# Weight preparation of a blockwise FFT convolution: ten transformed taps by TensorE, or seven by TensorE and three sums by VectorE

## The chip, the cores and the metric

One NeuronCore of a Trainium2 chip runs the whole program. The metric is the device time of one execution in microseconds (us). Engines are called as in the profile: PE is TensorE's matmul and PEld its weight load, DVE is VectorE, ACT is ScalarE, POOL is GpSimd, SP is SyncE, which issues the DMAs.

## The reference

A circular 7 x 7 convolution of a 224 x 224 image with 96 channels in and 96 out, written with FFTs. Input and output are bf16.

```python
wp = jnp.pad(w, ((0, H - K), (0, W - K), (0, 0), (0, 0)))
Xf = rfft2(x.astype(float32), axes=(1, 2))
Wf = rfft2(wp.astype(float32), axes=(0, 1))
Yf = jnp.einsum('bhwi,hwio->bhwo', Xf, Wf)
y = irfft2(Yf, s=(H, W), axes=(1, 2)).astype(bfloat16)
```

## The kernel before, in words

The kernel transforms the rows' axis only, in 8 blocks of 28 rows with windows of 34 (17 frequencies after a real DFT), and convolves directly along the columns, with 7 taps. The columns are worked in 7 tiles of 32 (16 even, 16 odd).

**Tables.** `WF[96 in, 50 slots, taps, 96 out]` holds the transformed weights. Frequency 0 has two slots, each other frequency three: parts 0 and 1 and their difference, part 2, so that a complex product takes three real ones. Even and odd columns are split in the same manner: the products need the even taps 0, 2, 4, 6, the odd taps 1, 3, 5, and the sums 0+1, 2+3, 4+5 (with 6). Before the change these sums are taps 7, 8 and 9 of the same table (`TAPS`, line 29).

**Weight preparation** (`prep_jobs`, lines 312 to 348) is done in groups of frequencies, `PGRP`. The raw weights `wq` are the stationary operand (98 rows: 49 taps by two halves of the output channels), and the moving operand is `Em`, a DFT table in which each column picks its slot and tap. One matmul gives, for one pair of output channels, all slots and taps of the group. Several of them fill a bank of PSUM (`pb`); one copy (CAST) then moves the bank into `WF`. For the groups after the first, TensorE makes parts 0 and 1 only, and `diff(s)` makes part 2 on VectorE, one TENSOR_TENSOR a frequency.

**Who copies.** `evac` (line 116) keeps a running cost for DVE and ACT and gives each copy to the engine with the lower sum; `diff` adds its cost to DVE's.

**Order.** Every engine runs its instructions in the order in which the program issues them (`_Ordered`). At the start come tile 0's row transform for frequencies 0 to 7, filler matmuls on `wu`, group 0's weights (`prep_jobs(0)`, line 679), then more of the row transform and the first J planes (`jit`, line 685). Then rounds r = 0 to 20 follow (line 727): in round r tile 0 works on frequency r and tile 1 on frequency r - 4. In `b_round` (line 466) a frequency goes like this:

- matmuls `pb<-WF,J` and `pb<-WF,xf` into bank b0 (19 of 96 columns), whose first four use taps 7, 8, 9, 6;
- ACT copies part of b0 to `tt_` (ACTIVATE), then DVE makes `u` from b0 and `tt_`;
- `mid()`: filler jobs; then 14 matmuls into bank b1; DVE makes `v`;
- J planes for three later frequencies on DVE, if due (three TENSOR_TENSOR: 1824, 456 and 912 elements);
- POOL (from tile 2 on sometimes DVE) adds v and u into `yf`; after planes, that sum waits for them; `end()`: filler jobs.

The filler jobs are the row transform of the next tiles and the weights of the next group: group g is spread over the rounds of the frequencies of group g - 1 (line 715), evenly by `pace`. `tt_`, u and v have two buffers each, and all matmul results share 8 PSUM banks, so PE can be only a few banks ahead of the copies. A group is due before the first of its frequencies is convolved.

After a tile's 17 frequencies, `yf` goes through DRAM (`scr`) and comes back transposed (`tt`); matmuls with `Gm` do the inverse DFT, ACT copies to `yo`/`J`, SP stores. From round 14 on no weights are prepared.

The tile's first pixels lie in the last slots of `WF` (`late`, line 155) until the last group's weights overwrite them.

Of the kernel before, what the change touches and what calls it, by code (L numbers as in the profile page):

```python
# [8 lines left out]
BF16 = mybir.dt.bfloat16  # L9
F32 = mybir.dt.float32  # L10
ALU = mybir.AluOpType
ACTF = mybir.ActivationFunctionType

KT = 7
# [8 lines left out]
TW = 16  # L23
HALO = 3
PXC = 16
NB = 8
POS = TW + HALO
NTAP = 10
TAPS = ((7, 8, 9, 6), (0, 2, 4, 6), (1, 3, 5))
NSLOT = 2 + 3 * (NS - 1)  # L30
PGRP = ((0, 2), (2, 5), (5, 8), (8, 11), (11, 14), (14, 17))
YGRP = ((0, 3), (3, 6), (6, 9), (9, 12), (12, 15), (15, 17))
YGRPL = ((0, 3), (3, 6), (6, 9), (9, 12), (12, 15), (15, 17))
SA = 9
# [13 lines left out]
def slot(s, part):  # L48
    return part if s == 0 else 2 + 3 * (s - 1) + part
# [3 lines left out]
def kernel(  # L53
# [7 lines left out]
    _, H, W, C = x.shape  # L61
# [4 lines left out]
    R = HB + PAD  # L66
# [3 lines left out]
    C2 = C // 2  # L70
# [21 lines left out]
    VE, SE, GE, TE, DE = (_Ordered(e) for e in (nc.vector, nc.scalar, nc.gpsimd, nc.tensor, nc.sync))  # L92

    cpool = ctx.enter_context(tc.tile_pool(name="const", bufs=1))
# [10 lines left out]
    load = {"v": 0.0, "a": 0.0}  # L105
# [3 lines left out]
    def apart(key, zone, r):  # L109
        for z, q in parts.setdefault(key, []):  # L110
            if z != zone and q.engine != r.ins.engine:
                tc.declare_no_dep(r.ins, q, reason="disjoint parts of one tile")
        parts[key].append((zone, r.ins))
        return r

    def evac(out_ap, in_ap, n):
        if tail[0]:
            return tail_evac(out_ap, in_ap, n)
        cv, ca = 180 + 1.0 * n, 160 + 0.85 * n
        if load["v"] + cv <= load["a"] + ca:  # L120
            load["v"] += cv
            return VE.tensor_copy(out=out_ap, in_=in_ap)
        load["a"] += ca
        return SE.copy(out=out_ap, in_=in_ap)
# [6 lines left out]
        return DE.dma_start(out=out_ap, in_=in_ap)  # L131

    WF = cpool.tile([128, NSLOT, NTAP, C], BF16, name="WF")
    PP = POS * NJ
    JN = 7 * 3 * PP
    J_bufs = [cpool.tile([128, JN], BF16, name=f"J{i}") for i in range(3)]
# [6 lines left out]
    XW = 2 * TW * C  # L143
# [8 lines left out]
    WC = C * C - C2  # L152
    Em = wqx[0:PW2, WC:WC + 2 * NSLOT * NTAP].rearrange("p (h a t) -> p h a t", h=2, a=NSLOT)
    XHW = PAD * C + 32
    late = WF[0:R, NSLOT - 8:NSLOT].rearrange("p a t o -> p (a t o)")
    x0_bufs = [late[:, i * (XW + 32):(i + 1) * (XW + 32)] for i in range(2)]
    xh_bufs = [late[:, 2 * (XW + 32) + i * XHW:2 * (XW + 32) + (i + 1) * XHW] for i in range(2)]
    assert 2 * (XW + 32 + XHW) <= 8 * NTAP * C and NSLOT - 8 > slot(PGRP[-1][0], 0)

    def load_rows(xb, jg, w0, npx):  # L160
        h0 = jg * HB - PAD
# [53 lines left out]
    twc = ftile([PW2, KT]); mf = ftile([R, JG, NS * 2])  # L215
# [31 lines left out]
    floor_div(GE, twp[:], pm[:], 2)  # L247
    GE.tensor_single_scalar(out=th14[:], in_=twp[:], scalar=-2.0, op=ALU.mult)
    GE.tensor_tensor(out=hf[:], in0=th14[:], in1=pm[:], op=ALU.add)
    GE.tensor_scalar(out=mk[:, 0:KT], in0=twc[:], scalar1=twp[:, 0:1], scalar2=None, op0=ALU.is_equal)  # L250
    GE.tensor_tensor(out=mk[:, KT:NTAP], in0=mk[:, 0:6:2], in1=mk[:, 1:6:2], op=ALU.add)
    GE.tensor_scalar(out=mk2[:, 1], in0=mk[:], scalar1=hf[:, 0:1], scalar2=None, op0=ALU.mult)
    GE.tensor_tensor(out=mk2[:, 0], in0=mk[:], in1=mk2[:, 1], op=ALU.subtract)
    for xb in xh_bufs:
# [3 lines left out]
    for xb in xf_bufs:  # L258
# [3 lines left out]
                     in1=mf.rearrange("p j (s r) -> p j s r", r=2), op=ALU.mult)  # L262
# [7 lines left out]
    for k0, k1 in ((0, slot(PGRP[0][1], 0)), (slot(PGRP[0][1], 0), NSLOT)):  # L270
        VE.tensor_tensor(out=Em[:, :, k0:k1], in0=pe3[:, k0:k1].unsqueeze(1).unsqueeze(3).to_broadcast([PW2, 2, k1 - k0, NTAP]),
                         in1=mk2[:].unsqueeze(2).to_broadcast([PW2, 2, k1 - k0, NTAP]), op=ALU.mult)
# [39 lines left out]
    def prep_jobs(gi):  # L312
        s0, s1 = PGRP[gi]
        ns = s1 - s0
        full = gi == 0
        ncol = (NSLOT_OF(s0, s1) if full else 2 * ns) * NTAP
        nb = C // NB
        hb = NB // 2
        assert NB * ncol <= 512 and C2 % hb == 0

        def mk_(ob):
            def f():
                pw = bank()
                pv_ = pw[:, 0:NB * ncol].rearrange("p (k h q) -> p k h q", h=2, q=ncol)
                ev = Em[:, :, slot(s0, 0):slot(s1 - 1, 2) + 1, :]
                ev = ev.rearrange("p h a t -> p h (a t)") if full else ev.rearrange("p h (s r) t -> p h s (r t)", r=3)[:, :, :, 0:2 * NTAP]
                for k in range(hb):
                    o = ob * hb + k
                    TE.matmul(pv_[:, k], lhsT=wqx[0:PW2, o:o + 127 * C + 1:C], rhs=ev, start=True, stop=True)
                pv_ = pv_[0:C]  # L330
                o0, o1 = ob * hb, (ob + 1) * hb
                wv = WF[0:C, slot(s0, 0):slot(s1 - 1, 2) + 1]
                if full:
                    wv = wv.rearrange("i a t (h o) -> i (a t) h o", h=2)
                    apart(("W", gi), ob, evac(wv[..., o0:o1], pv_.rearrange("i k h q -> i q h k"), NB * ncol))
                    return
                wv = wv.rearrange("i (s r) t (h o) -> i s (r t) h o", r=3, h=2)
                apart(("W", gi), ob, evac(wv[:, :, 0:2 * NTAP, :, o0:o1],
                      pv_.rearrange("i k h (s q) -> i s q h k", s=ns), NB * ncol))
            return f  # L340

        def diff(s):
            def f():
                load["v"] += 60 + C * NTAP / 1.92
                w0, w1, w2 = (WF[0:C, slot(s, r)].rearrange("i t o -> i (t o)") for r in range(3))
                VE.tensor_tensor(out=w2, in0=w0, in1=w1, op=ALU.subtract)
            return f
        return [mk_(ob) for ob in range(nb)] + ([] if full else [diff(s) for s in range(s0, s1)])

    def NSLOT_OF(s0, s1):  # L350
        return slot(s1 - 1, 2) + 1 - slot(s0, 0)
# [114 lines left out]
    def b_round(t, s, mid, end, ydve=False, planes=()):  # L466
# [14 lines left out]
        def conv(bank, col, m, part, add=False, both=False):  # L481
            pl = st[m][part] if s > 0 else (xv[:, 0, :, 0], Jb[:, 2:4], Jb[:, 0:2])[m][:, part]
            tp = TAPS[m]
            for k, tp_ in enumerate(tp):
                o, wv = bank[:, col:col + C], WF[0:C, slot(s, part), tp_, :]
                if both:
                    o, wv = bank[:, col:col + 2 * C].rearrange("p (m o) -> p m o", m=2), wv.unsqueeze(1).to_broadcast([C, 2, C])
                TE.matmul(o, lhsT=pl[:, (HALO - k) * NJ:(HALO - k) * NJ + 128], rhs=wv,
                          start=(k == 0 and not add), stop=(k == len(tp) - 1 and not both and m != 2 or not add and not both and k == len(tp) - 1))
# [3 lines left out]
        if s == 0:  # L493
# [4 lines left out]
            for mi, m in enumerate((2, 1)):  # L498
                for part in range(2):
                    conv(b1, (mi * 2 + part) * C, m, part)  # L500
            VE.tensor_tensor(out=yv.rearrange("p r m o -> p m r o"),
                             in0=tt_[:, 0:2 * C].rearrange("p (r o) -> p r o", o=C).unsqueeze(1).to_broadcast([128, 2, 2, C]),
                             in1=b1[:, 0:4 * C].rearrange("p (m r o) -> p m r o", m=2, r=2), op=ALU.add)
# [5 lines left out]
        else:  # L509
            v = tv_pool.tile([128, 2, 2, C], F32, name="v")  # L510
# [368 lines left out]
```

## Time and profile before

| What | Value |
|---|---|
| Runs | 279.18, 280.52, 283.91 us; median 280.52 |
| Span of the profiled execution | 279.9 us (first to last instruction; it is the only time of that execution) |
| Mean granted TensorE clock | 0.981 |
| Instructions | 12291 |
| `pb<-wq` matmuls | 240 of 98x120 and 48 of 98x100 (columns of the moving operand last) |
| CAST `WF<-pb` on ACT | 52 of 480 elements, mean 578 ns; 6 of 400, mean 495 ns |
| CAST `WF<-pb` on DVE | 8 of 480, mean 646 ns; 6 of 400, mean 571 ns |
| TENSOR_TENSOR `WF<-WF` (diff) on DVE | 15 of 960, mean 752 ns |
| TENSOR_TENSOR `J<-xf` in four runs of 304 | 7 of 1216, mean 831 ns |
| TENSOR_TENSOR `yf<-v,u` on POOL | 85 of 384 (f32 in), mean 1012 ns |
| First weight matmul, first convolution matmul | 17.49 us, 22.03 us |

Nearly all instructions carry line 85, a helper's, so groups are told apart by their tiles: `WF<-pb` is written out of PSUM, `pb<-wq` is the weight transform, `pb<-Fm,xn` the row transform. A row of the time order has start, length, engine, operation, tiles, shape, count, and in brackets the idle time before it with what ended that. Consecutive equal instructions are merged into one row, so a row's length divided by its count is less than one instruction's length where they overlap.

### The profile page before, as it was taken

The page shows a single profiled execution, that of the slowest core. Times are in us where ns is not written, and L with a number is a line of the kernel's source. Part 1 is how long each engine was busy: PE and PEld are TensorE (multiplying, and loading weights), DVE is VectorE, ACT ScalarE, POOL GpSimd, SP SyncE. Part 2 cuts the span into 40 slices and gives each one's busy share as a digit, 9 for nine tenths or more (in the row PEclk, how much of TensorE's full clock was granted, in tenths as well). Part 3 has the DMA queues.
Part 4 walks back from the last instruction along what each step waited for, and adds up shares of the span by engine and source line. Part 5 has one row for each costly group of instructions (what it writes and reads, how often), then busy time and mean ns, then how long its engine had stood idle before and what let it go on. Part 6 is the DMA issues. An engine that isn't in the chain of part 4 may idle for free. (4 is left out here: it accounts for less than half of the span.)

```text
span 279.9 us, 12291 instructions
## 1 busy us (share of the span) xinstructions
PE 266.0 (95%) x5226; PEld 243.6 (87%) x5226; DVE 218.9 (78%) x457; ACT 199.0 (71%) x489; POOL 98.1 (35%) x146
## 2 busy tenths in 40 slices
PE   8989999999999999999999999999999996999791
PEld 3769999999999999999999999999999896989571
DVE  6547999889798798879887887789788798588232
ACT  5439996687964667988988699887989864574022
POOL 7720132453446654224223334322422333133000
PEclk9999999999999999999999999999999999799797
DMA  6947010812111597897977596989299339756935
GB/s 184 213 108 205 11 47 2 248 52 85 44 47 46 163 261 143 251 251 208 263 192 222 143 298 183 266 247 298 82 204 281 114 108 207 204 158 164 251 65 165
DMA packets 46038, 46.79 MB, mean 167 GB/s; under 512 B 35150, under 2 KB 36954, under 8 KB 45886
## 3 DMA queue, kind: packets, MB, share of 16 engines
q1 hardware_dynamic: 43696, 43.94, 57.9%
q10 hardware_dynamic: 2288, 2.06, 2.6%
q8 instruction: 41, 0.67, 1.1%
q14 instruction: 13, 0.11, 0.1%
HBM read 24.65 MB, written 21.33 MB: 164 GB/s over the span
## 5 line engine op out<-in xcount | busy, mean ns | idle before, releaser
L85 PE MATMUL pb<-WF,J 96*128 96x96 bf16 x2898 | 168.4, 206 | 0.9 <-DVE WF L85 0.3
L85 PEld LDWEIGHTS <-J 96*128 96x128 bf16 x2898 | 143.0, 98 | 10.6 <-issue 1.5
L85 POOL TENSOR_TENSOR yf<-v,u 128x384 bf16<-128x384 f32 x85 | 84.6, 1012 | 150.0 <-issue 102.0
L85 ACT CAST xf<-pb 96x408 bf16<-96x408 f32 (+2 forms) x147 | 68.5, 486 | 6.7 <-PE pb L85 4.6
L85 PE MATMUL pb<-WF,xf 96*128 96x96 bf16 x952 | 60.6, 207 | 1.2 <-DVE WF L85 0.6
L85 DVE TENSOR_TENSOR J<-xf 96x1824 bf16<-96x1824 bf16 (+1 forms) x84 | 60.0, 753 | 0.1
L85 PEld LDWEIGHTS <-xf 96*128 96x128 bf16 x952 | 47.4, 98 | 1.6 <-issue 1.0
L85 PE MATMUL pb<-Fm,xn 118*128 118x136 bf16 (+3 forms) x640 | 45.7, 199 | 0.4 <-DVE u L85 0.4
L85 PE MATMUL pb<-tt,Gm 102*84 102x384 bf16 (+1 forms) x132 | 32.8, 329 | 2.2 <-DMA tt<-scr 2.2
L85 ACT CAST WF<-pb 96x480 bf16<-96x480 f32 (+1 forms) x58 | 28.5, 569 | 6.8 <-PE pb L85 6.7
L85 ACT CAST J<-pb 84x384 bf16<-84x384 f32 (+1 forms) x66 | 28.3, 482 | 6.1 <-PE pb L85 3.1
L85 PEld LDWEIGHTS <-xn 118*128 118x128 bf16 x640 | 30.5, 97 | 0.5 <-issue 0.5
L85 ACT CAST yo<-pb 84x384 bf16<-84x384 f32 (+1 forms) x66 | 28.1, 480 | 4.0 <-PE pb L85 3.9
L85 DVE TENSOR_TENSOR J<-J 96x912 bf16<-96x912 bf16 (+1 forms) x42 | 25.0, 595 | 0.0
L85 PE MATMUL pb<-wq 98*128 98x120 bf16 (+1 forms) x288 | 21.5, 226 | 0.9 <-DMA wq<-in_w_dram 0.9
L85 PE MATMUL pb<-wu 128*128 128x512 bf16 (+1 forms) x80 | 20.2, 422 | 1.0 <-DVE ct L85 1.0
L85 PEld LDWEIGHTS <-wq 98*128 98x128 bf16 x288 | 19.5, 151 | 1.3 <-DMA wq<-in_w_dram 1.3
L85 PEld LDWEIGHTS <-wu 128*128 128x128 bf16 (+1 forms) x80 | 10.4, 132 | 9.7 <-issue 3.5
L85 DVE TENSOR_TENSOR yf<-v,u 128x384 bf16<-128x384 f32 x27 | 15.5, 574 | 0.9
L85 PEld LDWEIGHTS <-Gm 102*84 102x84 bf16 (+1 forms) x132 | 11.1, 118 | 3.0 <-DMA tt<-scr 2.4
L85 DVE CAST WF<-pb 96x480 bf16<-96x480 f32 (+1 forms) x14 | 8.1, 614 | 7.0 <-PE pb L85 6.9
L85 ACT CAST tt<-pb 112x384 bf16<-112x384 f32 x8 | 3.6, 480 | 11.9 <-PE pb L85 11.8
(391 smaller groups left out, 236.2 us busy)
## 6 DMA issues: line engine op xcount, KB each, us to landing
scr<-yf SPq DMA_DIRECT2D x30, 288.0 KB
xn<-in_x_dram SPq DMA_DIRECT2D x12, 672.0 KB
tt<-scr SPq DMA_DIRECT2D x24, 336.0 KB
out_dram<-yo SPq DMA_DIRECT2D x12, 252.0 KB
out_dram<-J SPq DMA_DIRECT2D x12, 252.0 KB
tt<-scr SPq DMA_DIRECT2D x6, 288.0 KB
wq<-in_w_dram SPq DMA_DIRECT2D x1, 1719.0 KB
WF<-in_x_dram SPq DMA_DIRECT2D x2, 672.0 KB
```

Source lines behind the costliest of these rows:

```text
L85: r = fn(*a, **k)
```

## The change

TensorE transforms 7 taps instead of 10: `Em`, `WF` and the group tables shrink, and a bank of PSUM holds more channels or more frequencies. The groups become 2, 3, 4, 4 and 4 frequencies instead of 2, 3, 3, 3, 3 and 3. The matmuls per bank are set by group (`HBK`: 6, 6, 4, 4, 4 instead of 4), the banks per group become 8, 8, 12, 12 and 12 instead of 12 each. The three sums go to a table of their own, `WS`, by one TENSOR_TENSOR a frequency on VectorE (`tapsum`), which follows that frequency's `diff`: 864 elements, 576 for frequency 0. The convolution reads taps 7 to 9 from `WS`. The overlay `late` moves to the last 12 slots. `tapsum` adds its cost to the running cost by which `evac` chooses.

```diff
-NB = 8
-NTAP = 10
+NTAP = 7
+NSUM = 3
-PGRP = ((0, 2), (2, 5), (5, 8), (8, 11), (11, 14), (14, 17))
+PGRP = ((0, 2), (2, 5), (5, 9), (9, 13), (13, 17))
+HBK = (6, 6, 4, 4, 4)
...
+    WS = cpool.tile([128, NSLOT, NSUM, C], BF16, name="WS")
...
-    late = WF[0:R, NSLOT - 8:NSLOT].rearrange("p a t o -> p (a t o)")
+    late = WF[0:R, NSLOT - 12:NSLOT].rearrange("p a t o -> p (a t o)")
...
-    GE.tensor_scalar(out=mk[:, 0:KT], in0=twc[:], scalar1=twp[:, 0:1], scalar2=None, op0=ALU.is_equal)
-    GE.tensor_tensor(out=mk[:, KT:NTAP], in0=mk[:, 0:6:2], in1=mk[:, 1:6:2], op=ALU.add)
+    GE.tensor_scalar(out=mk[:], in0=twc[:], scalar1=twp[:, 0:1], scalar2=None, op0=ALU.is_equal)
...
-        nb = C // NB
-        hb = NB // 2
-        assert NB * ncol <= 512 and C2 % hb == 0
+        hb = HBK[gi]
+        nb = C2 // hb
+        assert 2 * hb * ncol <= 512 and C2 % hb == 0
...
-        return [mk_(ob) for ob in range(nb)] + ([] if full else [diff(s) for s in range(s0, s1)])
+
+        def tapsum(s):
+            def f():
+                a0, a1 = slot(s, 0), slot(s, 1 if s == 0 else 2) + 1
+                load["v"] += 60 + (a1 - a0) * C * NSUM / 1.92
+                VE.tensor_tensor(out=WS[0:C, a0:a1], in0=WF[0:C, a0:a1, 0:2 * NSUM:2], in1=WF[0:C, a0:a1, 1:2 * NSUM:2], op=ALU.add)
+            return f
+        jobs = [mk_(ob) for ob in range(nb)]
+        for s in range(s0, s1):
+            jobs += ([] if full else [diff(s)]) + [tapsum(s)]
+        return jobs
...
-                o, wv = bank[:, col:col + C], WF[0:C, slot(s, part), tp_, :]
+                o, wv = bank[:, col:col + C], WF[0:C, slot(s, part), tp_, :] if tp_ < NTAP else WS[0:C, slot(s, part), tp_ - NTAP, :]
```

More of the change, by code (lines that the diff above doesn't have):

```diff
@@ L154 @@
     XHW = PAD * C + 32
-    late = WF[0:R, NSLOT - 8:NSLOT].rearrange("p a t o -> p (a t o)")
+    late = WF[0:R, NSLOT - 12:NSLOT].rearrange("p a t o -> p (a t o)")
     x0_bufs = [late[:, i * (XW + 32):(i + 1) * (XW + 32)] for i in range(2)]
     xh_bufs = [late[:, 2 * (XW + 32) + i * XHW:2 * (XW + 32) + (i + 1) * XHW] for i in range(2)]
-    assert 2 * (XW + 32 + XHW) <= 8 * NTAP * C and NSLOT - 8 > slot(PGRP[-1][0], 0)
+    assert 2 * (XW + 32 + XHW) <= 12 * NTAP * C and NSLOT - 12 >= slot(PGRP[-1][0], 0)
     def load_rows(xb, jg, w0, npx):
@@ L323, in f @@
                 pw = bank()
-                pv_ = pw[:, 0:NB * ncol].rearrange("p (k h q) -> p k h q", h=2, q=ncol)
+                n = 2 * hb * ncol
+                pv_ = pw[:, 0:n].rearrange("p (k h q) -> p k h q", h=2, q=ncol)
                 ev = Em[:, :, slot(s0, 0):slot(s1 - 1, 2) + 1, :]
@@ L334, in f @@
                     wv = wv.rearrange("i a t (h o) -> i (a t) h o", h=2)
-                    apart(("W", gi), ob, evac(wv[..., o0:o1], pv_.rearrange("i k h q -> i q h k"), NB * ncol))
+                    apart(("W", gi), ob, evac(wv[..., o0:o1], pv_.rearrange("i k h q -> i q h k"), n))
                     return
@@ L338, in f @@
                 apart(("W", gi), ob, evac(wv[:, :, 0:2 * NTAP, :, o0:o1],
-                      pv_.rearrange("i k h (s q) -> i s q h k", s=ns), NB * ncol))
+                      pv_.rearrange("i k h (s q) -> i s q h k", s=ns), n))
             return f
```

## The prediction

> **What bounds the kernel now.** I read the page's first part, then busy time by stretches, then the time order of single engines. The first part:
>
> ```profile
> PE 266.0 (95%) x5226; PEld 243.6 (87%) x5226; DVE 218.9 (78%) x457; ACT 199.0 (71%) x489; POOL 98.1 (35%) x146
> ```
>
> TensorE (PE) is busy for 95% of the span, so a matmul less is time less wherever nothing else is late. VectorE's 78% is a mean. The stretches in which the weights are prepared (width, then busy us of PE, weight load, DVE, ACT, POOL, then clock):
>
> ```profile
> 30.00:50.00 20.00, 19.07 (x457) 18.77 (x457) 19.73 (x36) 16.63 (x43) 5.90 (x6) 1.00 0.11 35
> 50.00:82.00 32.00, 32.00 (x734) 31.91 (x732) 27.41 (x54) 24.39 (x57) 13.91 (x15) 1.00 0.29 93
> 82.00:97.00 15.00, 14.92 (x397) 14.78 (x394) 12.29 (x29) 8.81 (x23) 10.18 (x12) 1.00 0.24 76
> ```
>
> From 30 to 50 us DVE is busy 19.73 of 20 us, more than PE. From 50 to 82 us PE is full and DVE has 4.6 us idle. The time order of PE, in the places the change touches:
>
> ```profile
> 17.49 3.15 PE L85 MATMUL pb<-wq 98*128 98x100 bf16 x48 [0.87 <-DMA wq<-in_w_dram]
> ...
> 22.38 1.45 PE L85 MATMUL pb<-wq 98*128 98x120 bf16 x20
> ...
> 24.07 0.76 PE L85 MATMUL pb<-WF,J 96*128 96x96 bf16 x14
> ```
>
> ```profile
> 41.97 0.33 PE L85 MATMUL pb<-WF,xf 96*128 96x96 bf16 x4 [0.36 <-DVE WF L85]
> ...
> 46.73 0.55 PE L85 MATMUL pb<-Fm,xn 118*128 118x32 bf16 x16 [0.38 <-DVE u L85]
> ```
>
> One matmul lasts about 0.2 us but the next starts long before its end. The last two rows carry the forecast: at 41.97 and 46.73 PE stands and waits for DVE. And DVE, from which the rest is priced:
>
> ```profile
> 28.70 1.21 DVE L85 CAST WF<-pb 96x480 bf16<-96x480 f32 x2
> 29.95 1.79 DVE L85 TENSOR_TENSOR WF<-WF 96x960 bf16<-96x960 bf16 x3
> 31.66 0.54 DVE L85 SCALAR_TENSOR_TENSOR v<-tt__643,pb 128x384 f32<-128x384 f32 x1
> 32.12 1.41 DVE L85 TENSOR_TENSOR J<-xf 96x1824 bf16<-96x1824 bf16 x2
> 33.45 0.62 DVE L85 TENSOR_TENSOR J<-J 96x912 bf16<-96x912 bf16 x1
> ...
> 40.51 2.55 DVE L85 TENSOR_TENSOR WF<-WF 96x960 bf16<-96x960 bf16 x3
> ...
> 43.91 1.96 DVE L85 TENSOR_TENSOR J<-xf 96x1824 bf16<-96x1824 bf16 x2
> ...
> 46.34 0.34 DVE L85 SCALAR_TENSOR_TENSOR u<-pb,tt__1130 128x192 f32<-128x192 f32 x1
> ```
>
> ```profile
> 40.40 1.00 POOL L85 TENSOR_TENSOR yf<-v,u 128x384 bf16<-128x384 f32 x1 [3.92 <-DVE J L85]
> 43.60 0.99 POOL L85 TENSOR_TENSOR yf<-v,u 128x384 bf16<-128x384 f32 x1 [2.20 <-DVE v L85]
> ```
>
> No DVE row from 29.95 to 48.49 us has idle time before it: it is one unbroken chain. The same three differences take 1.79 us at 29.95 and 2.55 at 40.51, where POOL's sum is running; the two J rows take 1.41 and, beside the next POOL sum, 1.96.
>
> **The change part by part.** Counts are from the instruction order of the two built kernels.
>
> *TensorE.* Each group has 48 matmuls, and six groups become five: 288 become 240. At 100 columns they start (3.15-0.22)/47 = 62 ns apart, at 120 columns (1.45-0.23)/19 = 64 ns, where 0.22 is one matmul's length; the convolution's 96 columns take (0.76-0.21)/13 = 42 ns. So the width does not set the 62 ns, and I give nothing for 70, 84 or 112 columns: 48 x 62 ns = -3.0 us. Bounds: 42 ns each, -2.0; or also 10 ns less on the 96 narrow ones, -4.0. Groups 0 to 2 keep 48 matmuls each, at the same times, so the saving falls after round 5 (47 us).
>
> The Trainium skill (TensorE: Matmul & The Clock Gate, Back-to-back issue gap) has the gap follow the columns, N/2.4 + 2.5 ns; by it the estimate would be 14.7 us before, 10.4 after, -4.3. The rows above contradict it: 100 and 120 columns cost the same.
>
> *VectorE, new prices.* Bf16 sums: 1.10 us for 1824 elements, 0.39 for 456, 0.65 for 960, so 0.52 ns an element; 672 elements (a difference now) 0.50, 864 (a tap sum) 0.60. Independent ones start 0.07 to 0.08 us before the end of the one ahead ((1.79-0.65)/2 = 0.57 apart). A tap sum reads the difference just ahead of it, and such a reader starts after the end: the casts that began at 28.70 ended at 29.91, the difference started at 29.95. So a pair takes 0.50 + 0.03 + 0.52 = 1.06 us where a difference took 0.57. Bounds for the tap sum, whose rows of 96 lie apart: 0.60 by the dense rows, and 1.02 at the rate of v and u (0.54 and 0.35 us for 384 and 192 elements, 0.99 ns each). Taken: 0.60, since J with four separate runs of 304 (1216 elements) has a mean of 0.83. Casts cost (1.21-0.65) = 0.57 apart at 480 elements, 0.54 at 448.
>
> *Rounds 1 to 5, on the path.* Between v at 31.66 and u at 46.34 DVE gets four casts of 0.54 for two of 0.57 (+1.0) and, in round 4, four pairs for three differences (4.24 - 1.71 = +2.5): 3.5 us. Beside POOL it already loses 0.76 + 0.55 us; I keep that. Bounds: 1.8 (no wait inside a pair, one collision less), 5.2 (the dear tap sum). The chain's start: DVE now adds two tap sums (0.37 + 0.52) behind the last cast before J, a third xf copy goes to ACT, and the first convolution starts about 0.6 later; round 1 then has one cast and three pairs (0.60 + 3.2) for four casts and three differences (2.3 + 1.7) and the 1.60 us that DVE waited for ACT at 28.43. I get v at 28.43 + 0.9 + 0.27 + 2.1 = 31.7, unchanged (plus or minus 0.5). Behind the pairs stand u, v and J of the next rounds. PE waits on that u at 46.73 with no slack, so PE is late by **+3.5**.
>
> *Rounds 5 to 13.* DVE loses two casts, one xf copy and nine differences (1.1 + 0.6 + 5.1) and gets eight pairs (8.5): +1.6. Its idle time there is 0.3 + 4.6; with PE 3.0 faster 1.9 stays, so the pairs just fit. Taken **+0.3**; bounds 0, and 2.0 for new collisions.
>
> The Trainium skill (GPSIMD Engine Reference, Specifications) says that GpSimd shares its SBUF interfaces with VectorE and contends with instructions that have two SBUF inputs. The 2.55 row agrees, and it speaks against 32 such instructions in place of 15; a full sum's wait for each new one would be an estimate of 17 us, none would be 0.
>
> *Edits at nothing.* ACT has 43 casts for 58, and is nowhere PE's releaser there. The shorter weight table product (1.1 us) and the longer zero fill lie before 17.46 us, where PE waits for the weights' DMA: that cover holds as long as both end before it. SP's order of DMAs is unchanged, so no queue moves; POOL's two memsets (0.19 and 0.28) come two sums earlier, under its idle time. After round 13 nothing differs.
>
> *Sum.* 279.9 span - 3.0 + 3.5 + 0.3 = 280.7. The median of the runs, 280.52, is 0.6 above this span (runs 279.18 to 283.91), so the forecast for a median is **281.3**, no change.
>
> **The rivals.**
> 1. PE's saving shows. If the pairs have no inner wait, the chain starts 0.5 earlier and a collision goes, u is late by 1.3 instead of 3.5: 279.1. For it: ACT and DVE together lose 15 + 5 casts. Against it: DVE has no idle between 29.95 and 48.49.
> 2. Slower: collisions with POOL's sums in rounds 7 to 12. Each difference or tap sum that starts behind a v falls on a 1.0 us POOL sum and loses up to 0.76. With 1.9 - 1.6 = 0.3 us spare, it decides from the second collision on; eight pairs give 8 x 0.76 = 6.1, less 0.8 already paid (the nine differences there have the row mean 0.75, not 0.65): 286.6. Against it: a DVE that waits for PE before u meets POOL already done.
> 3. Tap sums at one element a cycle: 0.42 each, four before u and eight behind: +5.0, 286.3. The J row with four runs speaks against it.
> 4. The clock drops. After PE's one wait of 2.2 us for tt at 236.75 the granted clock read 0.64 and 0.51 from 238 to 242; a wait of 3 us at 42 to 47 might do the same: about 3.4 us at half speed, +1.7, 283.0. The shorter waits at 41.97 and 46.73 left it at 1.00.
>
> **How the numbers follow.** Forecast 0.45, rival one 0.22, two 0.13, three 0.07, four 0.13. The likeliest case alone spans 279.7 to 282.9. The range 278.3 to 285.5 leaves out rival three, half of two and the far end of one, below 0.2. Two per cent (274.9 and 286.1) is about what a measurement of this kernel can tell from no change. Faster by that needs more than the 4.0 us that PE can save: 0.03. Slower: most of three, half of two: 0.13. Within: 0.84.
>
> **What would show it.** 240 matmuls on wq, about 62 ns apart; pairs 1.06 us apart; the u behind the fourth group of J rows near 50 us and PE's wait in front of it 3 to 4 us instead of 0.5; from 50 to 85 us PE gaining 3 us. Wrong would be: wq matmuls below 55 ns, tap sums over 0.75 us, DVE with idle time between 32 and 48 us, or a clock under 1.00 near 50 us.

## The result, and the profile after

The changed kernel takes **292.25 us** (median of 4 runs, 291.33 to 293.69) against 280.13 us before (4 runs, 279.18 to 283.91): 1.043 times as long, 95% interval 1.039 to 1.048. The forecast was 281.3 us, no change, with a range to 285.5. The profiled execution has a span of 290.9 us and took 292.58 us. Medians in this document are over all runs of a kernel, ratios leave out those over 1.5% above its fastest and compare with runs of the kernel before taken alongside (medians 280.8 to 281.5 us), and a profile is of one run, for instance in e8 the fastest, in e4, e9 and e16 the slowest of its kernel.

The first part of the page of the changed kernel, and its row of the TensorE clock in 40 slices of 7.3 us:

```profile
PE 267.1 (92%) x5178; PEld 245.8 (85%) x5178; DVE 225.5 (78%) x467; ACT 194.1 (67%) x476; POOL 97.8 (34%) x145
...
PEclk9997996895997899999999999999999999999998
```

The shares look almost as before: DVE at 78% again, PE three points lower. What is new stands in the second row: the clock dips four times in the first 14 slices, where before it dipped in none. The same stretches as in the prediction show where (columns as there, the clock behind the five engines):

```profile
30.00:50.00 20.00, 16.74 (x393) 16.43 (x390) 19.48 (x36) 14.07 (x37) 4.22 (x4) 0.90 0.05 18
50.00:82.00 32.00, 29.36 (x606) 29.22 (x604) 24.00 (x48) 19.82 (x47) 10.99 (x11) 0.85 0.27 84
82.00:97.00 15.00, 10.50 (x208) 10.36 (x205) 14.19 (x27) 4.65 (x13) 6.03 (x7) 0.78 0.11 42
```

PE was full from 50 to 97 us before; now it lacks 7.1 us of 47, and what it does there is partly done at half clock (0.85 and 0.78). DVE is nearly unbroken from 82 to 97 us, and yet has 8 us idle from 50 to 82.

In the time order of PE four waits stand out; the brackets have the idle time before the row and what ended it:

```profile
44.35 0.30 PE L86 MATMUL pb<-WS,J 96*128 96x96 bf16 x3 [1.62 <-DVE WS L86]
...
48.25 1.28 PE L86 MATMUL pb<-WF,J 96*128 96x96 bf16 x14 [1.63 <-DVE v L86]
...
67.02 0.42 PE L86 MATMUL pb<-WS,J 96*128 96x96 bf16 x3 [2.63 <-ACT xf L86]
...
91.95 0.42 PE L86 MATMUL pb<-WS,J 96*128 96x96 bf16 x3 [4.50 <-DVE J L86]
```

Three such matmuls take 0.30 us at 44.35 and 0.42 at 67.02 and 91.95, fourteen take 1.28 us at 48.25 (0.76 before): half clock. The row at 67.02 names ACT, but the matmul reads J planes, and the second row of planes on DVE (456 elements, merged into the "x2" row at 65.55) ends at 66.9. What DVE did before 91.95:

```profile
84.42 0.54 DVE L86 SCALAR_TENSOR_TENSOR v<-tt__1938,pb 128x384 f32<-128x384 f32 x1
84.89 0.35 DVE L86 SCALAR_TENSOR_TENSOR u<-pb,tt__1994 128x192 f32<-128x192 f32 x1
85.15 1.35 DVE L86 TENSOR_TENSOR WS<-WF 96x864 bf16<-96x864 bf16 x1
86.43 0.49 DVE L86 TENSOR_TENSOR WF<-WF 96x672 bf16<-96x672 bf16 x1
86.96 0.60 DVE L86 TENSOR_TENSOR WS<-WF 96x864 bf16<-96x864 bf16 x1
87.48 0.54 DVE L86 SCALAR_TENSOR_TENSOR v<-tt__1994,pb 128x384 f32<-128x384 f32 x1
87.95 0.35 DVE L86 SCALAR_TENSOR_TENSOR u<-pb,tt__2050 128x192 f32<-128x192 f32 x1
88.21 1.25 DVE L86 TENSOR_TENSOR WF<-WF 96x672 bf16<-96x672 bf16 x1
89.50 0.60 DVE L86 TENSOR_TENSOR WS<-WF 96x864 bf16<-96x864 bf16 x1
90.02 0.54 DVE L86 SCALAR_TENSOR_TENSOR v<-tt__2050,pb 128x384 f32<-128x384 f32 x1
90.49 1.40 DVE L86 TENSOR_TENSOR J<-xf 96x1824 bf16<-96x1824 bf16 x2
```

```profile
85.04 1.00 POOL L86 TENSOR_TENSOR yf<-v,u 128x384 bf16<-128x384 f32 x1 [1.97 <-DVE v L86]
88.11 0.99 POOL L86 TENSOR_TENSOR yf<-v,u 128x384 bf16<-128x384 f32 x1 [2.06 <-DVE v L86]
```

The bunch of a group's pairs stands in front of v and of the J planes. An instruction of a pair that starts just after GpSimd has begun a sum takes 1.25 to 1.35 us instead of 0.49 to 0.60; it ends 0.4 to 0.5 us after that sum's end. PE is meanwhile as far ahead as the planes allow, and stands still for 4.5 us.

In the rest of the text, as in the expectations, a wait of PE is counted from the start of its last matmul, which makes it 0.2 us longer than the idle time in the brackets (1.8, 1.8, 2.8 and 4.7 us here).

**Where the time went.** VectorE makes one v per frequency and tile, so the n-th v is the same instruction in all kernels. The 1st, 5th, 21st and 35th v start at 31.66, 46.60, 81.70 and 105.61 us before. I call the stretches between them *rounds 1 to 5*, *rounds 5 to 13* and *behind*. "Late" is the delay of the 35th v ("at 118 us" in the expectations below) against the first profile of before; the delay then stays within 0.7 us until 232 us. A second profile of each of the two kernels is in the table too.

| Late by (us) | start | rounds 1 to 5 | rounds 5 to 13 | behind | 35th v |
|---|---|---|---|---|---|
| before again (b2) | -0.25 | 0.0 | 0.0 | 0.0 | -0.2 |
| changed | 1.2 | 3.4 | 7.5 | 2.7 | 14.9 |
| changed again (a2) | 1.1 | 3.4 | 8.0 | 2.8 | 15.4 |
| no sums (e1) | 0.0 | 1.0 | -1.6 | 0.4 | -0.2 |
| groups of three (e2) | 1.6 | 1.6 | 7.3 | 1.6 | 12.1 |
| pairs in time (e3) | 0.3 | 2.7 | 3.6 | 3.0 | 9.5 |
| filled waits (e4) | 1.1 | 3.4 | 6.3 | 0.8 | 11.6 |
| half the sums (e8) | -0.3 | 2.2 | 1.4 | 1.9 | 5.2 |
| GpSimd copies (e10) | 0.8 | 2.4 | 6.6 | 1.5 | 11.3 |
| pairs ahead of the sum (e12) | -0.2 | 3.6 | 1.4 | 3.7 | 8.4 |
| before in that order (e13) | -0.7 | 2.7 | -0.8 | 2.3 | 3.6 |
| e12, half the sums (e16) | -1.1 | 2.3 | 0.6 | 3.0 | 4.7 |
| e12, no sums (e15) | -0.4 | 0.2 | -2.6 | 2.0 | -0.7 |

Rounds 5 to 13 hold eight pairs wherever VectorE makes all sums (nine in e2). In e3, e6, e7, e12, e13, e15 and e16 two or three pairs or differences move into the stretch "behind", which makes it longer.

Of the 14.9 us, 3.9 are not in the span. That goes with the clock records of the 20 profiles: between 232 us and the last half clock, which ends each run, both profiles of before have two pieces of 3.41 us at half clock and the changed kernel's first has none. The eleven profiles with none regain 3.9 to 5.9 us there, the six with one piece 1.8 to 3.4, the two with two nothing, and e4 with three loses 1.0. With the second profiles (293.5 and 279.8 us) the difference is 13.7. I therefore judge mechanisms by the table, which repeats within 0.6 us, and the time by medians.

### The profile page after: what moved, and what is told of

It is laid out like the page before. It is cut to its first block, busy times and chain, and to the rows that moved or that the text cites. A ratio compares the mean times of both kernels' runs of the same rounds, so it can differ in the third digit from the quotient of the medians.

```text
span 290.9 us, 12194 instructions
## 1 busy us (share of the span) xinstructions
PE 267.1 (92%) x5178; PEld 245.8 (85%) x5178; DVE 225.5 (78%) x467; ACT 194.1 (67%) x476; POOL 97.8 (34%) x145
## 4 chain that ended last, share of the span: by engine, by line
PE 70%; DVE 12%; DMA 9%; ACT 4%; issue 2%; SPq 1%; DVEq 0%; ACTq 0%
PE pb L86 70%; DMA wq<-in_w_dram 5%; DVE J L86 3%; DVE v L86 2%; ACT xf L86 2%; DVE WF L86 2%; DVE WS L86 2%; DMA xf<-scrb 2%; DMA tt<-scr 2%; DVE u L86 1%; DVE yf L86 1%; ACT WF L86 1%; DMA scrb<-yf 1%; SPq L86 1%; DVE xf L86 0%
## 5 line engine op out<-in xcount | busy, mean ns | idle before, releaser
L86 PE MATMUL pb<-WF,J 96*128 96x96 bf16 x2562 | 162.4, 209 | 2.0 <-DVE v L86 1.6
L86 PEld LDWEIGHTS <-J 96*128 96x128 bf16 x2898 | 146.3, 99 | 20.6 <-DVE J L86 7.7
L86 ACT CAST xf<-pb 96x408 bf16<-96x408 f32 (+3 forms) x149 | 69.2, 483 | 7.3 <-PE pb L86 5.4
L86 PE MATMUL pb<-WS,xf 96*128 96x96 bf16 x714 | 56.4, 209 | 1.5 <-ACT ct L86 1.4
L86 PE MATMUL pb<-WF,xf 96*128 96x96 bf16 x238 | 45.7, 209 | 0.0
L86 PE MATMUL pb<-WS,J 96*128 96x96 bf16 x336 | 33.5, 209 | 8.8 <-DVE J L86 4.5
L86 ACT CAST WF<-pb 96x448 bf16<-96x448 f32 (+2 forms) x43 | 20.7, 546 | 8.8 <-PE pb L86 8.7
L86 PE MATMUL pb<-wq 98*128 98x112 bf16 (+2 forms) x240 | 18.5, 239 | 1.1 <-DMA wq<-in_w_dram 1.1
L86 PE MATMUL pb<-wu 128*128 128x512 bf16 (+1 forms) x80 | 17.8, 385 | 1.0 <-DVE ct L86 1.0
L86 PEld LDWEIGHTS <-wq 98*128 98x128 bf16 x240 | 17.1, 156 | 1.5 <-DMA wq<-in_w_dram 1.5
```

Source lines behind the costliest of these rows:

```text
L86: r = fn(*a, **k)
```

## The experiments

Theory at the start: the tap sums on VectorE hold up v, u and the J planes, PE waits, and each wait halves the clock. First rival: not the sums but the regrouping to four frequencies does it.

**e1_no_sums**, the sums left out.

```diff
-        jobs = [mk_(ob) for ob in range(nb)]
-        for s in range(s0, s1):
-            jobs += ([] if full else [diff(s)]) + [tapsum(s)]
-        return jobs
+        return [mk_(ob) for ob in range(nb)] + ([] if full else [diff(s) for s in range(s0, s1)])
...
-                o, wv = bank[:, col:col + C], WF[0:C, slot(s, part), tp_, :] if tp_ < NTAP else WS[0:C, slot(s, part), tp_ - NTAP, :]
+                o, wv = bank[:, col:col + C], WF[0:C, slot(s, part), tp_ if tp_ < NTAP else 2 * (tp_ - NTAP), :]
```

> The changed kernel with its 17 tap sums left out: the convolution reads taps 0, 2 and 4 of WF in the place of the sums, so that part of the computation is missing. Theory: the sums on VectorE, issued in front of v, u and the J planes, cause PE's four long waits (1.8, 1.8, 2.8 and 4.7 us at 42.5, 46.4, 64.2 and 87.3 us), and each wait is followed by a half clock. Without the sums I expect no PE wait above 1 us from 30 to 97 us, a granted clock of 1.00 there and 276 to 279 us (280.1 before, less the 3.0 us of matmuls). Rival, the regrouping: four differences in one bunch and banks of another size hold up the rounds by themselves; then 285 us or more.

277.17 us (10 runs), 0.992 of before (0.986 to 0.997); clock 1.00 from 20 to 110 us, longest wait there 1.2 us (1 expected). The sums are the cause, not the regrouping.

**e2_groups_of_three**, the sums kept, the old groups.

```diff
-PGRP = ((0, 2), (2, 5), (5, 9), (9, 13), (13, 17))
-HBK = (6, 6, 4, 4, 4)
+PGRP = ((0, 2), (2, 5), (5, 8), (8, 11), (11, 14), (14, 17))
+HBK = (6, 6, 6, 6, 6, 6)
...
```

> The changed kernel with the groups of frequencies of before (2, 3, 3, 3, 3, 3; six matmuls to a bank, 8 banks a group), sums kept. PE gets its 48 matmuls back (+3.0 us). Theory (the sums): the waits remain, in shorter bunches of three pairs, 286 to 294 us, a clock below 1.00 in at least one stretch between 30 and 97 us. Rival (the regrouping): 280 to 283 us with the clock at 1.00.

291.79 us, 1.041 (1.031 to 1.052), four half-clock stretches of 3.4 us between 47 and 99 us: the theory again. PE waits in more and shorter pieces, six of 0.8 to 1.4 us.

**e3_pairs_in_time**, one pair a round.

```diff
...
+    later = []
     for gi in range(1, len(PGRP)):
-        add(2 * PGRP[gi - 1][0], 2 * PGRP[gi - 1][1] - 1, prep_jobs(gi))
+        banks, prs = prep_jobs(gi)
+        a = 2 * PGRP[gi - 1][0]
+        b = max(2 * PGRP[gi - 1][1] - 2, a + 3)
+        add(a, b, banks)
+        later += [(max(2 * s - 2, b - 1), p) for s, p in prs]
+    for k, p in later:
+        add(k, k + 1, p)
```

> The changed kernel with the same work, but difference and tap sum of a frequency s are issued in round s-1, one pair a round, in place of all pairs of a group in the last rounds of the group before; the last three pairs so move behind round 12. Theory, refined: it is the bunching in front of the J planes that makes the waits. Then no PE wait above 2 us from 30 to 97 us, at most one half-clock stretch, 278 to 283 us. Rival: the amount of VectorE work in rounds 1 to 13 counts and not where it stands; then PE's waits come elsewhere and the time stays above 288 us.

287.18 us, 1.028 (1.017 to 1.038), between the two, with waits of 2.7 and 2.2 us, where I expected none above 2, and two half-clock stretches, where I expected at most one. Rounds 5 to 13 lose 3.6 us instead of 7.5: the bunches cost about 4. But a pair now starts behind u in each round, beside a sum of GpSimd, and its rows, with those of J, are 8.0 us longer than the shortest of their kind (changed kernel 5.4).

**e4_filled_waits**, filler matmuls in front of four banks.

```diff
+FILL = {(0, 5, 0): 8, (0, 5, 1): 8, (0, 9, 0): 12, (1, 9, 0): 20}
...
+    def fill_wait(b, key):
+        for _ in range(FILL.get(key, 0)):
+            TE.matmul(b[:].rearrange("p (a b) -> p a b", a=4), lhsT=wu[:, 0:128], rhs=wur, start=True, stop=True)
...
+            fill_wait(b0, (t, s, 0))
...
+            fill_wait(b1, (t, s, 1))
```

> The changed kernel with filler matmuls on wu (512 columns) in front of the four convolution banks at which PE waited (8, 8, 12 and 20 of them, each about 0.22 us), written into the bank that the convolution then overwrites. The waits stay, the clock should not drop. Theory: of the 14.9 us by which the changed kernel is late at 118 us, some 7 to 8 come from matmuls at half clock after the waits (by the spacing of matmuls in the four stretches); 283 to 287 us and a clock of at least 0.97 in each stretch from 30 to 97 us. Rival: VectorE sets the pace there whatever PE's clock is, and the half clock costs only what it would have waited anyway; then 290 to 293 us with the clock at 1.00.

293.10 us, 1.049 (1.039 to 1.058). Two of its stretches:

```profile
50.00:82.00 32.00, 30.79 (x670) 29.01 (x668) 25.33 (x49) 20.35 (x48) 12.03 (x12) 1.00 0.27 85
82.00:97.00 15.00, 14.37 (x276) 11.90 (x273) 13.88 (x29) 5.00 (x14) 6.38 (x9) 1.00 0.11 42
```

The clock stays at 1.00 and the 35th v is still 11.6 us late, so the half clock was worth at least 3.3 to 3.8 us by then, where I expected 7 to 8: 1.2 to 1.8 in rounds 5 to 13 and about 2 behind. It can be more, because not all fillers fit into the waits: the eight in front of the second bank write into that bank and start only when it is free, at 48.16, so that its own matmuls start at 49.88, 1.7 us late; at 91.04 they start 0.5 us behind the planes. The end gives the gain back: three pieces at half clock behind 232 us, the first of them after a wait for tt of 2.1 us.

Now the theory was: the sums, their bunches, their collisions and the clock together. Is VectorE simply full?

**e5_sums_on_gpsimd**

```diff
-                load["v"] += 60 + (a1 - a0) * C * NSUM / 1.92
-                VE.tensor_tensor(out=WS[0:C, a0:a1], in0=WF[0:C, a0:a1, 0:2 * NSUM:2], in1=WF[0:C, a0:a1, 1:2 * NSUM:2], op=ALU.add)
+                GE.tensor_tensor(out=WS[0:C, a0:a1], in0=WF[0:C, a0:a1, 0:2 * NSUM:2], in1=WF[0:C, a0:a1, 1:2 * NSUM:2], op=ALU.add)
```

> The changed kernel with the 17 tap sums on GpSimd in place of VectorE; the cost that they add to VectorE's running sum goes too. Theory: VectorE's time in rounds 1 to 13 is what is short; without the sums there 279 to 283 us, PE's waits from 30 to 97 us below 1.5 us each. Rival (GpSimd's sums hold up VectorE's sums with two SBUF operands, which took 1.28 to 1.35 us instead of 0.60 beside a 1.0 us sum of GpSimd): 16 more sums on GpSimd, estimated at 1.0 to 2.2 us each by its 2.6 ns an element of float32, hold differences and J planes up for about as long as they last; then 288 to 300 us.

303.22 us, 1.075 (1.068 to 1.082): the rival. Groups of its profile (busy us, mean ns, then idle before):

```profile
L86 POOL TENSOR_TENSOR WS<-WF 96x864 bf16<-96x864 bf16 x16 | 33.3, 2096 | 6.0 <-DVE WF L86 5.5 <-issue 0.5
...
L86 DVE TENSOR_TENSOR WF<-WF 96x672 bf16<-96x672 bf16 x15 | 16.2, 1103 | 0.3 <-ACT WF L86 0.3
```

A sum takes 2.1 us there, and a difference 1.10 (0.66 in the changed kernel). VectorE's sums of two SBUF operands are 19.5 us longer in all than if each took the shortest time of its kind (changed kernel 5.4): work moved to GpSimd came back to VectorE as waiting.

**e6_ten_taps_four**: PE transforms all ten taps, in the new groups.

```diff
+PGRP = ((0, 2), (2, 5), (5, 9), (9, 13), (13, 17))
+HBK = (4, 4, 3, 3, 3)
...
```

with each difference issued as in e3.

> The kernel before, all ten taps transformed by TensorE, with the changed kernel's groups of 2, 3, 4, 4 and 4 frequencies (240 matmuls instead of 288; 160 columns for the groups of four, three matmuls to a bank, 16 banks a group), and each difference issued in round s-1 in place of the end of the group. VectorE does no tap sums. Theory: the width of these matmuls does not set their 62 ns and VectorE has the time for the differences: PE saves up to 3.0 us, 277 to 279 us. Rival (160 columns cost in proportion to the width against 96 columns in 42 ns, 70 ns each): 144 x 8 ns = 1.2 us of the gain is lost, and 16 banks in place of 12 of the same size per group add nothing; 278.5 to 280 us. If bunches of casts from four-frequency groups hold VectorE up, 281 us or more.

290.61 us, 1.034 (1.025 to 1.043), most likely for another reason. ACT is nearly full, 29.01 of 32 us (24.39 before):

```profile
50.00:82.00 32.00, 28.06 (x604) 27.05 (x602) 26.32 (x50) 29.01 (x49) 11.93 (x12) 1.00 0.26 84
...
L86 ACT CAST WF<-pb 96x480 bf16<-96x480 f32 x49 | 41.7, 1015 | 0.0
```

Of these 49 casts, the seven of the group with four matmuls to a bank take 0.56 to 0.61 us, as before; the 42 of the groups with three, which write runs of three channels, take 0.91 to 1.39, 1.09 on average. At 160 columns the wq matmuls start 74 ns apart (median; 62 at 120). So the width does count beyond 120 columns.

**e7_no_sums_in_time**: e1 and e3 together.

> The changed kernel without its tap sums (the convolution reads taps 0, 2 and 4 in their place, that part of the computation is missing) and with each difference issued in round s-1. Without the sums and with four differences in a bunch, the rounds up to 118 us were 0.2 us early, not 3.0. Theory: the bunches of four differences (PE waits of 0.9, 1.1, 1.2 and 0.8 us there) ate the 3.0 us; with one difference a round the rounds at 118 us are 2 to 3.5 us early, and the time is 1.5 to 3 us below that of the kernel with the sums left out alone. Rival: the saving is lost to something else (the start, the clock); then no difference over 0.7 us.

278.15 us, 0.988 (0.981 to 0.995), not better than e1, 0.4 us late. The theory fell: differences in this place collide too (7.8 us longer than their shortest with the J rows, 3.5 in e1), and two of them now stand behind the 21st v, in a stretch that takes 1.7 us more (0.4 in e1).

**e8_half_the_sums**

```diff
-            jobs += ([] if full else [diff(s)]) + [tapsum(s)]
+            jobs += ([] if full else [diff(s)]) + [tapsum(s)] * (s % 2)
...
```

> The changed kernel with the tap sums of the odd frequencies only (8 of 17); for the even ones the convolution reads taps 0, 2 and 4 in their place, so that part is missing. Theory with a threshold (VectorE's idle time takes up the first sums, as the prediction had it for all): late by at most 3 us at 118 us, and at most one half-clock stretch between 30 and 97 us; 278 to 281.5 us. Rival (each sum stands in front of something PE waits for, from the first): half of the 15.1 us between none and all, so 7 to 8 us late at 118 us, 283 to 287 us.

284.44 us (10 runs, 280.97 to 287.58), 1.007 (1.002 to 1.013); 5.2 us late, between both expectations. Eight of the 17 sums cost 5.4 of the 15.1 us, in the fastest of the ten runs: there is no free first half.

**e9_differences_first**

```diff
-        for s in range(s0, s1):
-            jobs += ([] if full else [diff(s)]) + [tapsum(s)]
-        return jobs
+        if not full:
+            jobs += [diff(s) for s in range(s0, s1)]
+        return jobs + [tapsum(s) for s in range(s0, s1)]
```

> The changed kernel with all differences of a group issued ahead of its tap sums, in place of difference and sum in pairs. The work and the rounds are the same, but a sum no longer reads the result of the instruction just ahead of it: such a reader starts 0.03 us after the end, an independent one 0.08 us before it. Theory: the price is 0.11 us for each of 15 pairs, 1.6 us, and VectorE sets the pace, so 289.5 to 292 us and 13 to 14.5 us late at 118 us. Rival: the wait inside the pair is lost in PE's waits; 292 to 293.5 us.

291.10 us, 1.036 (1.028 to 1.045), 15.8 us late in its profile, which is of a run of 294.08 us where the other three took 290.8 to 291.2. The median is 1.2 us under that of the changed kernel, the runs overlap: whether the wait inside the pair counts is not settled.

**e10_no_second_input**

```diff
+                if t < 2:
+                    return eng.tensor_copy(out=yv.rearrange("p r m o -> p m r o"), in_=v[:])
```

> The changed kernel in which GpSimd only copies v into yf for the first two tiles, so that the addition of u is left out there. It tells what the collisions of VectorE's SBUF sums with GpSimd's cost. In the changed kernel they make VectorE's differences, tap sums and J rows 5.4 us longer between 29 and 100 us than the shortest of their kind (before: 3.2 us). Theory (the amount of VectorE work leads, the collisions add to it): if a copy does not hold VectorE up, 9 to 12 us late at 118 us, 286.5 to 290 us. Rival (the collisions decide): at most 4 us late, below 283 us. If copies hold VectorE up as sums do, nothing changes.

288.43 us, 1.023 (1.015 to 1.031), 11.3 us late: as the theory said. GpSimd's copy takes 0.51 us instead of 1.00, and VectorE's sums lose 1.7 us instead of 5.4. Collisions are worth 3.6 to 4.1 us, not the whole.

**e11_casts_to_scalar**

```diff
-BIAS = 3000.0
+BIAS = 15000.0
```

> The changed kernel with the start value of VectorE's running cost raised (BIAS 15000 for 3000): nine casts of rounds 1 to 4 (five of WF, four of xf, 0.54 to 0.60 us apart, 5.1 us in all) go from VectorE to ScalarE, which has 6 us idle from 30 to 50 us. Theory: VectorE is what is short in these rounds, so v of round 5 (51.3 us, 4.7 us late) comes 3 to 5 us earlier, and the waits of 1.8 us at 42.5 and 46.4 us shrink; 287 to 290 us. Rival: the later rounds limit it anyway and take the gain back; 291 to 293 us.

293.59 us, 1.039 (1.027 to 1.051), 16.1 us late. VectorE is 5.1 us lighter from 30 to 50 us (14.39 us busy) and the 5th v is 1.5 us later than in the changed kernel:

```profile
39.44 0.36 DVE L86 SCALAR_TENSOR_TENSOR u<-pb,tt__892 128x192 f32<-128x192 f32 x1 [3.38 <-ACT tt__892 L86]
39.89 0.56 DVE L86 SCALAR_TENSOR_TENSOR v<-tt__892,pb 128x384 f32<-128x384 f32 x1
42.06 1.41 DVE L86 TENSOR_TENSOR J<-xf 96x1824 bf16<-96x1824 bf16 x2 [1.62 <-ACT xf L86]
```

It waits 3.4 and 1.6 us for ACT, whose `tt_` now stands behind the casts, and the four pairs and planes follow as before. The theory did not come true, but the run does not part amount from place either: ScalarE, without idle time from 35.5 to 45.0 us, became what VectorE waits for.

**a2_changed_again**, the same kernel.

> The changed kernel once more, for a second profile of it. If the four half-clock stretches and the four waits belong to the change, they are here at the same rounds within 1 us, and the rounds at 118 us are 14 to 16 us late; if chance set them, their number differs. In the last 50 us PE's wait for the tt DMA (1.5 us in the first profile of the changed kernel, 2.4 us before) is expected to differ by chance, between 0.8 and 2.4 us over the profiles so far, and a half clock to follow it only from 2.0 us on.

293.5 us span. The four long waits are at 42.4, 46.2, 64.4 and 87.6 us with 1.8, 1.9, 2.8 and 4.7 us, and a half clock follows at 46.7, 67.2 and 91.1: they belong to the change. The first half clock of the changed kernel does not keep its place: at 25.6 us there, at 19.4 here. The guess on the tt wait failed: here a half clock follows a wait of 1.7 us.

Open at that point: place (e3), collisions (e10) and clock (e4) each explained 3 to 5 of some 15 us. Are place and collisions the whole, or does the bare amount of VectorE's work remain?

**e12_pairs_ahead_of_sum**: one pair a round, issued like J planes ahead of GpSimd's sum, which waits for it; where a half round already has planes, half a round earlier.

```diff
...
+        for s, p in prs:
+            pairs[(s - 2, 1) if s % 3 == 1 and s > 4 else (s - 1, 0)] = p
...
-            now = jit(*now) if now else ()
+            now = pairs.pop((r, t), []) + (jit(*now) if now else [])
```

> The changed kernel, one pair (difference and tap sum) a round, issued right behind a v and ahead of GpSimd's sum of that half round, which waits for the pair as it does for J planes; no half round has both J planes of the later rounds and a pair, three half rounds of the first four apart. Theory A (place and collisions are what cost): the collisions fall from 5.4 us to at most 3, no PE wait above 1.5 us from 30 to 97 us, no half clock there, at most 5 us late at 118 us, 280 to 284 us. Theory B (VectorE's amount of work: per round two u and two v 1.5 us, two thirds of a J group 1.5, a pair 1.05, together 4.05 us, with PE's round at 4.0): it stays 7 us late or more, 285 to 288 us.

286.17 us (6 runs: three near 284.6, of which the profile is one, and three near 288), 1.027 (1.017 to 1.037). VectorE at 63 us, and PE's next row:

```profile
63.15 0.53 DVE L86 SCALAR_TENSOR_TENSOR v<-tt__1548,pb 128x384 f32<-128x384 f32 x1
63.61 0.83 DVE L86 TENSOR_TENSOR WF<-WF 96x672 bf16<-96x672 bf16 x1
64.47 0.60 DVE L86 TENSOR_TENSOR WS<-WF 96x864 bf16<-96x864 bf16 x1
65.00 0.35 DVE L86 SCALAR_TENSOR_TENSOR u<-pb,tt__1599 128x192 f32<-128x192 f32 x1
...
65.13 0.29 PE L86 MATMUL pb<-WS,J 96*128 96x96 bf16 x3 [1.76 <-DVE WS L86]
```

A difference now loses 0.3 us, not 0.8; collisions are down to 3.75 us, near the 3.2 of before. The rounds 5 to 13 lose 1.4 us, but PE still waits 2.0 us there and again at 86.1 us, one half clock follows, and the 35th v is 8.4 us late: nearer to theory B. Both waits, and two of 1.9 and 1.6 us at 31.1 and 41.1, end with a tap sum that PE's next matmuls read (64.47 to 65.07, PE at 65.13). A pair is issued here only about a round ahead of its use, so place still costs something in this order; one pair a round but issued earlier was not tried.

**e13_before_diffs_ahead**: the kernel before in that order.

> The kernel before with each difference issued a round ahead, behind a v and ahead of GpSimd's sum, which waits for it; ten taps and groups of three as before. Its differences and J rows lose 3.2 us to collisions and PE waits 0.5 us each at 41.4 and 46.2 us. If PE's bound holds (95% busy), at most 1 us is gained: 0 to 1 us early at 118 us, 279 to 281.5 us. If placement matters here too, 2 us early or more.

284.72 us, 1.012 (1.001 to 1.023), 3.6 us late. Both expectations missed: it gains 0.75 us in rounds 5 to 13, but loses 2.7 in rounds 1 to 5, where the first differences come too late (PE waits 1.3 us at 30.8 and 1.7 us at 39.4), and 2.3 behind, where three of them now stand.

**e14_planes_earlier**

```diff
-            bursts[(g0 - 2, 1 if g0 - 2 >= LAG else 0)] = (0, g)
+            bursts[(g0 - 2, 0)] = (0, g)
...
-        bursts[(r1, 0 if r1 < NS else 1)] = (1, g)
+        bursts[(r1, 0) if g == 0 else (r1 - 1, 1)] = (1, g)
```

> The changed kernel with the J planes of all later groups issued half a round earlier, so ahead of some of the pairs behind which they stood; the work is the same. If it is the J planes that PE waits for and the pairs could come later, the waits of 2.8 and 4.7 us at 64.2 and 87.3 us shrink to below 2 and the rounds at 118 us are 9 to 12 us late, 286 to 289.5 us. If VectorE's work as a whole is late, PE waits as long for something else, 14 us late or more, 291 to 294 us.

290.05 us, 1.039 (1.031 to 1.046), 13.0 us late. The two long waits become 2.0 and 0.6 us, but new ones of 1.9 us (69.7) and 0.9 and 1.1 us (92.1 and 95.5) take their place. Whatever stands behind the pairs is late.

**b2_before_again**

> The kernel before once more, for a second profile of it. Rounds up to 118 us within 1 us of the first profile; PE's wait for the tt DMA in the last 50 us between 0.8 and 2.4 us by chance, and a half clock behind it only from 2.0 us on, so that the span can be 279.9 or up to 4 us less.

279.8 us, all rounds within 0.25 us of the first profile. The wait for tt is 1.96 us, and the half clock comes only at 259.4.

**e15_ahead_no_sums** and **e16_ahead_half_sums**: e12 without sums, and with those of the odd frequencies.

> The kernel with one pair a round ahead of GpSimd's sum, without its tap sums (the convolution reads taps 0, 2 and 4 in their place, so that part is missing); what stays is its order of the differences. By the kernel before in this order (3.6 us late at 118 us) less the 3.0 us of matmuls: 0 to 2 us late, 276.5 to 280 us. If the order alone made the 8.7 us it stays at 5 or more.

> The same with the sums of the odd frequencies only (8 of 17; the convolution reads taps 0, 2 and 4 for the even ones, that part is missing). If VectorE's bare amount sets the pace and has idle time to use up first, the first eight sums cost less than the others: 1 to 3.5 us late at 118 us. If each sum costs the same (between the kernel without and the 8.7 us with all), 4 to 5.5 us.

e15: 275.56 us, 0.980 (0.973 to 0.987), 0.7 us early. e16: 282.41 us (10 runs), 1.002 (0.997 to 1.006), 4.7 us late. The first eight sums cost 5.4 us and the other nine 3.7: no idle time was used up first. In this order a sum costs 9.1/17 = 0.54 us on average, about its own length (0.60, or 0.53 from start to start); in the order of the changed kernel (14.9 + 0.2)/17 = 0.89. These are single profiles, and e12 and e16 have one half clock each between 60 and 70 us where e15 has none, so the near equality with a sum's own length is partly chance.

No kernel with complete sums came under the time before.

## Why the prediction was wrong, step by step

The forecast added 0.8 us to the span. The table has 1.2 + 3.4 + 7.5 + 2.7 = 14.9 us up to the 35th v (rounded), of which 3.9 come back behind 232 us: 11.0.

- *48 matmuls less, -3.0.* Right in kind and size: they start 61 to 63 ns apart (medians) at 70, 84 and 112 columns, and e15 shows -2.6 us in rounds 5 to 13 without the sums. The changed kernel never sees it. The formula of the Trainium skill (TensorE: Matmul & The Clock Gate, Back-to-back issue gap) that the prediction held against its rows is given there for a single matmul by itself, without its weight load, so the rows do not contradict the page.
- *The chain's start, v at 31.7, unchanged.* It came at 32.90 and 32.77: 1.2 us late, where 0.5 was allowed.
- *Rounds 1 to 5, +3.5.* They took +3.4, and u behind the fourth group of J rows came at 51.01, for "near 50". The pairs are 1.05 us apart (1.06 forecast), unhindered tap sums take 0.60. This price and this mechanism held; only PE's wait came in two parts of 1.8 us, at 42.5 and 46.4, and not as one of 3 to 4.
- ***Rounds 5 to 13, +0.3, bounds 0 and 2.0: "so the pairs just fit".* This is the step that failed.** With PE's -3.0 it gave -2.7; the measure is +7.5 and +8.0. Two things were wrong. The smaller is the amount: VectorE's busy time between the 5th and the 21st v rose by 3.8 us, from 30.24 to 34.06, not by 1.6, because the 16 instructions of the eight pairs took 12.8 us beside GpSimd's sums, where the shortest of their kind would take 8.8. By the prediction's own sum, 1.9 us of it to spare, that makes +1.9 in place of +0.3, and the stretch would still have been 1.1 us shorter than before. The larger is the spare time itself. VectorE had 4.85 us idle there, more than the 3.8 us added, and yet its idle time grew to 8.5 us. What I booked as spare time was eleven pieces of 0.1 to 0.8 us, each ahead of a u or a v, in which VectorE waited for PE, ACT or GpSimd. Work put in front of v does not use them: it makes v late, then PE, then VectorE waits for PE (1.6 us at 53.7; nine pieces of 0.4 to 0.8 us more up to 79.5, some of them for ACT or GpSimd). Best shown by e15, e16 and e12: -2.6, +0.6 and +1.4 us with no, half and all sums, so 4.0 us for the sums even in the better order, and VectorE is idle there for 5.0 us without sums and still for 4.6 with all. From there to the changed kernel's +7.5: e3's spreading alone brings +3.6 (bunches about 4), keeping clear of GpSimd's sums +1.4 (about 2); e4 prices the half clock within the two at 1.2 to 1.8 or more. These parts come from single profiles and need not add up exactly.
- *After round 13 nothing differs.* The instructions do not, but the stretch took 2.7 us more, since the fourth half clock reaches from 90.4 to 97.3 us; with the waits filled 0.8 remain.
- *Rival 2, collisions.* They came in part: 5.4 us against 3.2 before, so 2.2 more, where the forecast paid for none beyond those of before and the rival for 5.3. With GpSimd's sums made copies (e10) the 35th v comes 3.6 to 4.1 us earlier. *Rival 3* fell (0.60 us). *Rival 4, the clock, +1.7 for one stretch*: four stretches of 3.4, 6.8, 6.8 and 6.8 us came, three of them behind the long waits, and cost at least 3.3 to 3.8 by the 35th v. I had priced rivals 2 and 4 as alternatives, though both came at once, and had no case for a bunch in front of the J planes of the later rounds.
- *The base.* Each profiled run takes 1.7 us more than its span (292.58 and 290.9; 281.56 and 279.8), not 0.6; the first profile of before lay above its median. This is small beside the rest.

Not settled: why the waits behind 232 us, and with them the half clock there, differ from run to run; whether another order of the pairs could hide the sums; and e6's cast, where the run of three is the likely cause, since the same kernel's casts of 480 elements with runs of four were not slower, but was not tried apart from its group.

## What to carry to other kernels

When two engines feed each other in turn, the idle time of the second can be waiting for the first, as it was here: in every order tried, added work cost about its own length or more, from the first instructions on. Work that stands where the engine waits and nothing behind it is due should cost less; no run here shows such a place. Price it by what stands behind it in its queue, round by round, and not by busy time against a stretch. A bunch of such work in front of a buffer that TensorE needs turns into one long wait, and the wait into half clock.

## What the runs showed of the hardware

- **The clock follows pieces of 3.41 us, and a part of one idle is enough.** All half-clock stretches last a multiple of 3.41 us and lie on a grid of that step. I cut the 20 profiles into the pieces of their grid that lie between 18 and 262 us, and summed PE's idle time in each. Of pieces at full clock with 1.5 us idle or more, all 28 were followed by half clock; with 0.9 to 1.5 us, 11 of 35; with less, none of 1270. At half clock, all 23 pieces with over 0.3 us idle were followed by another, and 8 of 57 with less. It is the sum in a piece that counts: in e4 1.78 us idle up to 48.16 fell on the border of two pieces, 0.9 us in each, and the clock stayed at 1.00. The Trainium skill (TensorE: Matmul & The Clock Gate, HAM oscillation) gives the rule "no PE-idle gaps >~3.4µs"; here 1.5 us in one piece was always enough, less than half of that.
- **GpSimd beside two-input sums on VectorE.** The Trainium skill (SBUF — State Buffer, SBUF: two separate sides) says that the one that starts later waits for the other's whole instruction. The rows agree: 0.60 us became 1.28 to 1.35 beside a sum of 1.0, and in e5, with 17 more sums on GpSimd, 16 of them of 2.1 us, VectorE lost 19.5 us in all.
- **A cast that writes runs of three bf16** took 1.09 us on ACT at 480 elements (42 casts of e6), one with runs of four 0.56 to 0.61 in the same kernel.
- **wq matmuls** start 61 to 63 ns apart (medians) from 70 to 120 columns, and 74 at 160.
